# Turning LayerNorm rows and normalised queries with DMAs from on-chip memory instead of on TensorE, in the forward pairs of a linear-attention and gated-MLP training step

## The chip, the core and the metric

The kernel runs on one core of a Trainium2 chip. The metric is the device time of one execution in microseconds (us). A change of this kernel is told from no change at about 0.2%, some 2.2 us.

A core has five engines that work side by side and wait for each other through semaphores: TensorE (PE, with its weight loads shown as PEld), VectorE (DVE), ScalarE (ACT), GpSimd (POOL) and SyncE (SP). Here SP issues all DMAs, one after the other, in one queue: an issue that has to wait holds up the issues behind it.

## The reference

A forward pass of four layers and its backward pass, for 2048 tokens of width 512 in bf16. Layers 0 and 2 are linear attention with 32 heads of width 16, layers 1 and 3 a gated MLP of width 1376. Weights are shared between layers 0 and 2 and between layers 1 and 3.

```python
def _A_ref(x, wqkv, wo):
    q, k, v = ...                       # x @ wqkv, split into heads
    pq, pk = phi(q), phi(k)             # where(t > 0, t + 1, exp(t)) + 1e-6
    kv = jnp.einsum("bhsd,bhse->bhde", pk, v)
    z = jnp.einsum("bhsd->bhd", pk)
    num = jnp.einsum("bhqd,bhde->bhqe", pq, kv)
    den = jnp.einsum("bhqd,bhd->bhq", pq, z)[..., None] + 1e-6
    return (num / den reshaped to (B, S, D)) @ wo

def _B_ref(x, w_gate, w_up, w_down):
    g = x @ w_gate; u = x @ w_up
    return (_sigmoid(g) * u) @ w_down

x = x + _A_ref(_layernorm(x), A_wqkv, A_wo)
x = x + _B_ref(_layernorm(x), B_w_gate, B_w_up, B_w_down)
x = x + _A_ref(_layernorm(x), A_wqkv, A_wo)
x = x + _B_ref(_layernorm(x), B_w_gate, B_w_up, B_w_down)
```

The outputs are x and the gradients of x and of the five weight matrices.

## The kernel before

The 2048 tokens are 16 tiles of 128 (`st`, `NST` = 16). Each forward attention layer is done in `kq_fwd` up to its small matrix `M_sb`; what is left of it, the product of the normalised queries with `M_sb`, is woven into the MLP layer that follows, in `ab_fwd`. That function runs over pairs of tiles; its loop has `i` from 1 to 7 and `st = 2*i`, once for layer 1 and once for layer 3. The first pair stands ahead of the loop, written out tile by tile.

One round of the loop holds:

- `gu`, six times ("units" below): 8 matmuls on `wg` and 8 on `wu` for two 128-wide chunks of the MLP (the sixth has one chunk). They read `hT`, the LayerNorm rows of the pair turned so that the model width lies on the partitions. ScalarE takes two sigmoids from `g_ps` (into `ssd_t` and `oms`), DVE multiplies with `u_ps` into `hhT`, POOL writes the second half of `ssd_t`, and SP stores `ssd_t` to DRAM (`sv_ssd`) for the backward pass. `ssd_t` has five buffers in layer 1 and three in layer 3; the PSUM pools `g`, `u` and `t` have two banks each, `y` and `ln` one.
- `down_mm`, twice: 11 matmuls each, for the two tiles of the pair before.
- `attn_y(st + 2)` and `attn_y(st + 3)`: 4 matmuls each, of the turned queries `pqnT` with `M_sb`; DVE adds the result to `x`, and `ln_stats` (DVE, then three small operations on POOL) prepares the LayerNorm.
- `ln.apply(st + 2)` and `ln.apply(st + 3)`: ScalarE writes normalised rows into `hstage`, and SP stores both to DRAM (`sv_h`). `ln.stage_T` turns the two tiles with 8 TensorE transposes into a PSUM bank, and ScalarE copies them to `hT` for the next round.
- for the pair after the next: `pair_prod` (POOL), `pair_front1` and `pair_front2` (DVE: the denominators, their reciprocals and the normalised queries `pqnstage`, stored as `sv_pqn`) and `pair_front3`, 8 TensorE transposes and a ScalarE copy into `pqnT`.
- `after`: LayerNorm rows of the next layer, or the output. `trans`: DVE's block transposes of `hhT` into `tr_stg`, stored as `sv_hdd` and `sv_hdl`. `turn_weights`: transposing DMAs and stores for the weights of the backward pass, or their copies.

TensorE, ScalarE, DVE and POOL execute in the order in which the program is written. The SP queue alone is put in order by the scheduler of the language. Several helpers record operations for many callers; `transpose_blocks`, `evac_copy` and `ps_tile` are of this kind.

Of the kernel before, what the change touches and what calls it, by code (L numbers as in the profile page):

```python
# [9 lines left out]
BF16 = mybir.dt.bfloat16  # L10
# [12 lines left out]
P = 128  # L23
NST = S // P
NDC = D // P
# [363 lines left out]
def dram_batch(ap2d, b, nb=NB):  # L389
    return ap2d[batch_rows(b, nb), :].rearrange("(n p) d -> p n d", p=P)  # L390
# [141 lines left out]
class FwdLN:  # L532
# [10 lines left out]
        if st < NST:  # L543
            self.nmr[st] = ln_stats(self.k, self.k.xs[st][:], self.rstd(st), st < 1)

    def apply(self, st):
        if st >= NST:
            return
        k, nc, l = self.k, self.k.nc, self.l
        if st % 2 == 0:  # L550
            self.cur = k.lnres["stg"].tile([P, 2, D], BF16, name="hstage", tag="hstage")
        h_t = self.cur[:, st % 2, :]
        self.hs[st] = h_t
        ln_apply(k, k.xs[st][:], h_t, self.nmr.pop(st), self.rstd(st), st < 1)
        if st % 2 == 1:
            nc.sync.dma_start(out=dram_batch(k.sv[l]["h"], st // 2, 2), in_=self.cur[:])

# [341 lines left out]
def attn_fronts(k, A, pool, small):  # L899
    nc = k.nc  # L900
    sva = k.sv[A.l]
    cur, F_ = {}, {}
    A.F = F_

    def prod(st, eng=None):
        if st >= NST:
            return
        if st % 2 == 0:
            cur["prod"] = pool.tile([P, 2, D], BF16, name="prod2", bufs=1)
        F_[st] = dict(prod=cur["prod"][:, st % 2, :])  # L910
        (eng or nc.gpsimd).tensor_tensor(F_[st]["prod"], A.pq_all[:, st, :], A.zb[:], ALU.mult)

    def front1(st):
        if st >= NST:
            return
        F_[st]["den"] = small.tile([P, H], F32, name="den")
        nc.vector.tensor_reduce(F_[st]["den"][:], F_[st]["prod"].rearrange("p (h e) -> p h e", h=H), AX.X, ALU.add)

    def front2(st):
        if st >= NST:  # L920
            return
        if st % 2 == 0:
            cur["pqn"] = pool.tile([P, 2, D], BF16, name="pqnstage", bufs=2)
        f = F_[st]
        den = f["den"]
        f["pqn"] = cur["pqn"][:, st % 2, :]
        nc.vector.tensor_scalar(den[:], den[:], EPS, None, ALU.add)
        nc.vector.reciprocal(A.rden_all[:, st, :], den[:])
        nc.vector.tensor_tensor(f["pqn"].rearrange("p (h e) -> p h e", h=H),
                                A.pq_all[:, st, :].rearrange("p (h e) -> p h e", h=H),  # L930
                                A.rden_all[:, st, :].unsqueeze(2).to_broadcast([P, H, DH]), ALU.mult)
        if st % 2 == 1:
            nc.sync.dma_start(out=dram_batch(sva["pqn"], st // 2, 2), in_=cur["pqn"][:])

    def front3(st):
        if st >= NST:
            return
        f = F_[st]
        if st % 2 == 0:
            cur["T"] = pool.tile([P, 2, NDC, P], BF16, name="pqnT2", bufs=2)  # L940
        pqnT = cur["T"][:, st % 2, :, :]
        transpose_blocks(k, k.ps["ln"], pqnT, [f["pqn"][:, c * P:(c + 1) * P] for c in range(NDC)],
                         "scalar", tag="ln_tp")
        f["T"] = pqnT

    def pair_prod(i):
        if i >= NST // 2:
            return
        f = F_[2 * i] = dict(prod=pool.tile([P, 2, D], BF16, name="prod2", bufs=1))
        nc.gpsimd.tensor_tensor(f["prod"][:], A.pq_all[:, 2 * i:2 * i + 2, :],  # L950
                                A.zb[:].unsqueeze(1).to_broadcast([P, 2, D]), ALU.mult)

    def pair_front1(i):
        if i >= NST // 2:
            return
        f = F_[2 * i]
        f["den"] = small.tile([P, 2 * H], F32, name="den2", bufs=2)
        nc.vector.tensor_reduce(f["den"][:], f["prod"][:].rearrange("p n (h e) -> p (n h) e", h=H), AX.X, ALU.add)

    def pair_front2(i):  # L960
        if i >= NST // 2:
            return
        f = F_[2 * i]
        den = f["den"]
        pqn = pool.tile([P, 2, D], BF16, name="pqnstage", bufs=2)
        rden = A.rden_all[:, 2 * i:2 * i + 2, :].rearrange("p n h -> p (n h)")
        nc.vector.tensor_scalar(den[:], den[:], EPS, None, ALU.add)
        nc.vector.reciprocal(rden, den[:])
        nc.vector.tensor_tensor(pqn[:].rearrange("p n (h e) -> p (n h) e", h=H),
                                A.pq_all[:, 2 * i:2 * i + 2, :].rearrange("p n (h e) -> p (n h) e", h=H),  # L970
                                rden.unsqueeze(2).to_broadcast([P, 2 * H, DH]), ALU.mult)
        nc.sync.dma_start(out=dram_batch(sva["pqn"], i, 2), in_=pqn[:])
        f["pqn"] = pqn

    def pair_front3(i):
        if i >= NST // 2:
            return
        pqn = F_[2 * i]["pqn"]
        pqnT = pool.tile([P, 2, NDC, P], BF16, name="pqnT2", bufs=2)
        ps = ps_tile(k, "ln", [P, 2, NDC, P], BF16, "ln_tp")  # L980
        for j in range(2):
            for c in range(NDC):
                nc.tensor.transpose(ps[:, j, c, :], pqn[:, j, c * P:(c + 1) * P], k.ident[:])
        nc.scalar.copy(pqnT[:], ps[:])
        for j in range(2):
            F_[2 * i + j] = dict(T=pqnT[:, j, :, :])

    A.pair_prod, A.pair_front1, A.pair_front2, A.pair_front3 = pair_prod, pair_front1, pair_front2, pair_front3

    def attn_mm(st, bank="y"):  # L990
        if st >= NST:
            return
        pqnT = F_[st]["T"]
        y_ps = F_[st]["y"] = ps_tile(k, bank, [P, D], F32, "y_ps")
        for c in range(NDC):
            nc.tensor.matmul(y_ps[:], lhsT=pqnT[:, c, :], rhs=A.M_sb[:, c, :],
                             start=(c == 0), stop=(c == NDC - 1))

    def attn_add(st):
        if st >= NST:  # L1000
            return
        y_ps = F_.pop(st)["y"]
        res = k.xs[st][:] if A.x_src is None else A.x_src[:, st, :]
        nc.vector.tensor_tensor(k.xs[st][:], y_ps[:], res, ALU.add)
        A.ln.stats(st)

    def attn_y(st, bank="y"):
        attn_mm(st, bank)
        attn_add(st)

    A.attn_mm, A.attn_add = attn_mm, attn_add
    A.prod, A.front1, A.front2, A.front3, A.attn_y = prod, front1, front2, front3, attn_y
# [38 lines left out]
def ab_fwd(k, A, ln, fill, nxt=None, out_cb=None, bwd=None):  # L1051
# [3 lines left out]
    with ExitStack() as ctx:  # L1055
# [89 lines left out]
        A.pair_front1(2)  # L1145
        gu(1, 1, *CQUADS[1])
        ln.apply(3)
        A.pair_front2(2)
        A.pair_prod(3)
        down_mm(0)  # L1150
        gu(1, 1, *CQUADS[2])
# [5 lines left out]
        for i in range(1, NPAIR):  # L1157
            st = 2 * i
            last = i == NPAIR - 1
            nf = fill.share(i, NPAIR - 1)  # L1160

            def trs(n):
                for _ in range(min(n, len(pend))):
                    trans(*pend.pop(0))
            nt = 1 if i < NPAIR - 2 else 2
            gu(st, 2, *CUNITS[0])
            if l == 3 and i > 1:
                turn_weights()
            A.attn_y(st + 2, "t")
            A.pair_front1(i + 2)  # L1170
            after(st - 3)
            gu(st, 2, *CUNITS[1])
            A.attn_y(st + 3, "t")
            A.pair_front2(i + 2)
            trs(nt)
            fills((nf + 2) // 3)
            gu(st, 2, *CUNITS[2])
            if l == 3 or i % 2 == 0:
                turn_weights()
            if i > 1:  # L1180
                down_mm(st - 2)
            ln.apply(st + 2)
            if last:
                trans(NBLK - 1, 0)
            gu(st, 2, *CUNITS[3])
            if l == 3:
                turn_weights()
            down_mm(st - 1, "t")
            ln.apply(st + 3)
            A.pair_prod(i + 3)  # L1190
            fills(nf // 3)
            trs(nt)
            if last:
                trans(NBLK - 1, 1)
            gu(st, 2, *CUNITS[4])
            ln.stage_T([st + 2, st + 3], bank="t")
            A.pair_front3(i + 2)
            after(st - 2)
            gu(st, 2, *CUNITS[5])
            if l == 3:  # L1200
                turn_weights()
            fills((nf + 1) // 3, "vector")
            if l == 1 and last:
                nc.scalar.activation(k.tab[:], k.neg[:], ACT.Exp)
            if i % 2 == 1 and not last:
                pend += [(i // 2, g) for g in range(NG + 1)]
            if i == NPAIR - 3 and bwd is not None:
                bwd.load_g(0)
# [920 lines left out]
```

## Time and profile before

| | |
|---|---|
| median of three runs | 1115.92 us (1115.59 to 1117.04) |
| the profiled execution | 1115.54 us, span 1113.8 us, clock 0.998 |
| TensorE busy over the span | 98% |
| DVE, ACT, POOL busy | 65%, 44%, 42% |
| DMA | 265.63 MB, 238 GB/s on average |
| loop of layer 1 / of layer 3 | about 87 to 201 us / 280 to 396 us |
| 8 transposes of `hstage` or `pqnstage` on TensorE | the next operation starts 0.45 us later |
| SP's time for an issue of `sv_ssd` (median) | 0.36 us |
| DMA transposes in the kernel | all from DRAM: weights in the forward pass, `dqT_ld`, `pkT_ld`, `gT`, `p_set` and others in the backward pass |

In the timelines a line gives the start, the length, the engine, the line of the kernel, the operation, output and input. "SPq" lines are the issues of DMAs by SP, not the transfers. In tables of windows the columns are start and end, length, busy time of each engine with its number of instructions, the granted TensorE clock, the busy share of the DMA engines and the GB/s that they moved. The chain of waits of this profile is followed back only as far as 814 us.

### The profile page before, as it was taken

The page shows a single profiled execution, that of the slowest core. Times are in us where ns is not written, and L with a number is a line of the kernel's source. Part 1 is how long each engine was busy: PE and PEld are TensorE (multiplying, and loading weights), DVE is VectorE, ACT ScalarE, POOL GpSimd, SP SyncE. Part 2 cuts the span into 40 slices and gives each one's busy share as a digit, 9 for nine tenths or more (in the row PEclk, how much of TensorE's full clock was granted, in tenths as well). Part 3 has the DMA queues.
Part 4 walks back from the last instruction along what each step waited for, and adds up shares of the span by engine and source line. Part 5 has one row for each costly group of instructions (what it writes and reads, how often), then busy time and mean ns, then how long its engine had stood idle before and what let it go on. Part 6 is the DMA issues. An engine that isn't in the chain of part 4 may idle for free. (4 is left out here: it accounts for less than half of the span.)

```text
span 1113.8 us, 20048 instructions
## 1 busy us (share of the span) xinstructions
PE 1086.5 (98%) x7374; PEld 668.7 (60%) x7476; DVE 718.4 (65%) x1263; ACT 491.8 (44%) x914; POOL 467.9 (42%) x627
## 2 busy tenths in 40 slices
PE   7999999999999999999999999999999999999998
PEld 4467777546777754445666556544447756555587
DVE  7888897888678677767984640067678956632221
ACT  4776656556665623444643451234446513420001
POOL 3728776433766556774111430048771102420000
PEclk9999999999999999999999999999999999999999
DMA  7955767696776678976889978998868999958997
GB/s 218 320 173 164 206 192 216 197 257 208 210 230 201 205 223 303 299 242 227 245 247 272 255 218 279 282 311 259 221 204 232 272 263 264 258 188 278 271 264 165
DMA packets 353267, 265.63 MB, mean 238 GB/s; under 512 B 116304, under 2 KB 331792, under 8 KB 353168
## 3 DMA queue, kind: packets, MB, share of 16 engines
q1 hardware_dynamic: 353168, 264.35, 82.5%
q8 instruction: 58, 0.95, 0.3%
q14 instruction: 41, 0.34, 0.1%
HBM read 122.62 MB, written 119.47 MB: 217 GB/s over the span
## 5 line engine op out<-in xcount | busy, mean ns | idle before, releaser
L1717 PE MATMUL p_ps<-p_set,p_a 128*128 128x384 bf16 (+2 forms) x1792 | 264.4, 303 | 1.3 <-DMA p_set<-sv_hdd 0.8
L1717 PEld LDWEIGHTS <-p_a 128*128 128x128 bf16 x1792 | 168.8, 96 | 84.9 <-PE p_ps L1717 1.0
L1408 POOL TENSOR_TENSOR dd<-dhb,ssd 128x512 bf16<-128x512 bf16 x84 | 96.8, 1156 | 103.7 <-ACT dhb L1406 97.7
L1407 DVE TENSOR_TENSOR dd<-dhh_ps,ssd 128x512 bf16<-128x512 f32 x85 | 57.1, 678 | 120.6 <-ACT dhb L1406 116.4
L1432 PE MATMUL dh_ps<-wuT,dd 128*128 128x512 bf16 (+1 forms) x339 | 128.5, 379 | 1.2 <-DVE junk L1251 0.7
L1091 POOL TENSOR_TENSOR ssd_t<-hhT,oms 128x512 bf16<-128x512 bf16 (+1 forms) x92 | 99.7, 1091 | 59.5 <-DVE hhT L1090 33.0
L1432 PE MATMUL dh_ps<-wgT,dd 128*128 128x512 bf16 (+1 forms) x329 | 124.7, 379 | 0.1
L1432 PEld LDWEIGHTS <-dd 128*128 128x128 bf16 x680 | 66.3, 98 | 80.8 <-issue 1.5
L1406 ACT CAST dhb<-dhh_ps 128x512 bf16<-128x512 f32 x84 | 48.7, 588 | 116.8 <-PE dhh_ps L1400 105.4
L1732 DVE TENSOR_TENSOR dw_stg<-p_ps,dw_stg 128x384 bf16<-128x384 f32 (+2 forms) x76 | 32.2, 438 | 105.3 <-PE p_ps L1717 96.0
L1072 PE MATMUL g_ps<-hT,wg 128*128 128x256 bf16 (+1 forms) x792 | 92.8, 260 | 1.2 <-ACT hT L380 0.5
L1072 PE MATMUL u_ps<-hT,wu 128*128 128x256 bf16 (+1 forms) x792 | 92.8, 261 | 0.9 <-DVE hhT L1090 0.9
L1040 DVE STREAM_TRANSPOSE tr_stg<-dd 128x768 f32<-128x768 f32 (+1 forms) x62 | 86.9, 1438 | 4.9 <-DMA sv_hdd<-tr_stg 3.8
L1088 ACT ACTIVATE ssd_t<-g_ps 128x512 bf16<-128x512 f32 (+1 forms) x92 | 51.6, 561 | 78.5 <-PE g_ps L1072 57.4
L1090 DVE TENSOR_TENSOR hhT<-u_ps,ssd_t 128x512 bf16<-128x512 f32 (+1 forms) x92 | 57.8, 631 | 38.8 <-ACT ssd_t L1088 32.2
L1072 PEld LDWEIGHTS <-wg 128*128 128x128 bf16 x792 | 70.1, 98 | 20.8 <-issue 1.2
L1400 PE MATMUL dhh_ps<-gT,wdT 128*128 128x512 bf16 x299 | 77.0, 379 | 2.6 <-DVE dd L1407 1.9
L1107 PE MATMUL y_ps<-wd,hhT 128*128 128x512 bf16 (+1 forms) x337 | 77.7, 379 | 0.8
L1072 PEld LDWEIGHTS <-wu 128*128 128x128 bf16 x792 | 70.6, 98 | 8.4 <-issue 1.4
L1734 ACT CAST dw_stg<-p_ps 128x384 bf16<-128x384 f32 (+2 forms) x76 | 28.0, 385 | 84.5 <-PE p_ps L1717 81.1
L1400 PEld LDWEIGHTS <-wdT 128*128 128x128 bf16 x352 | 34.2, 98 | 43.8 <-issue 4.1
L517 POOL TENSOR_TENSOR rstd_all<-rstd_all,neghalf 128x1 f32<-128x1 f32 x64 | 38.0, 595 | 47.5 <-DVE rstd_all L516 42.9
(253 smaller groups left out, 1896.6 us busy)
## 6 DMA issues: line engine op xcount, KB each, us to landing
sv_hdd<-tr_stg SPq DMA_DIRECT2D x72, 384.0 KB, 4.7
p_set<-sv_hdd SPq DMA_DIRECT2D x18, 1536.0 KB, 7.0
sv_ssd<-ssd_t SPq DMA_DIRECT2D x74, 256.0 KB, 2.6
ssd<-sv_ssd SPq DMA_DIRECT2D x23, 768.0 KB, 5.3
h_ld<-sv_h SPq DMA_DIRECT2D x30, 256.0 KB, 4.1
sv_hdl<-tr_stg SPq DMA_DIRECT2D x24, 256.0 KB, 4.9
p_a<-sv_h SPq DMA_DIRECT2D x12, 512.0 KB, 6.4
p_set<-sv_hdl SPq DMA_DIRECT2D x24, 256.0 KB, 5.1
```

The source lines that it names most:

```text
L1040: nc.vector.transpose(t[:, :, 0:n * P].bitcast(F32).rearrange("p q (a j) -> p q a j", a=2 * n), src.rearrange("p c x -> p (c x)").bitcast( ...
L1072: nc.tensor.matmul(ps[:, ci * n:(ci + 1) * n], lhsT=w_sb[:, kc, (c0 + ci) * P:(c0 + ci + 1) * P], rhs=hT[:, kc, (st % 2) * P:(st % 2) * P ...
L1088: nc.scalar.activation(ssd[:, :, 0, :], gv, ACT.Sigmoid)
L1090: nc.vector.tensor_tensor(hh, uv, ssd[:, :, 0, :], ALU.mult)
L1091: nc.gpsimd.tensor_tensor(ssd[:, :, 1, :], hh, oms, ALU.mult)
L1107: nc.tensor.matmul(y_ps[:], lhsT=h[0:r, fc, off:off + P], rhs=k.wd[0:r, fc, :], start=(fc == 0), stop=(fc == NFC - 1))
L1400: nc.tensor.matmul(ps[:], lhsT=k.wdT[:, jc, u * P:(u + 1) * P], rhs=self.gT[B][:, jc, :], start=(jc == 0), stop=(jc == NDC - 1))
L1406: nc.scalar.copy(dhb[:], ps[:])
L1407: nc.vector.tensor_tensor(self.dd[ng][:, 0, c, :], ps[:], self.ssd[ng][:, c, 0, :], ALU.mult)
L1408: nc.gpsimd.tensor_tensor(self.dd[ng][:, 1, c, :], dhb[:], self.ssd[ng][:, c, 1, :], ALU.mult)
L1432: nc.tensor.matmul(self.acc[j][:], lhsT=dd[0:r, a, c, j * P:(j + 1) * P], rhs=w[0:r, u, :], start=(u == 0 and a == 0), stop=(u == NFC - 1 ...
L1717: nc.tensor.matmul(ps[:, 0:w], lhsT=lhs[:, s, ic * P:(ic + 1) * P], rhs=rhs, start=(s == 0), stop=(s == NST - 1))
```

## The change

In the loop of `ab_fwd` the turning of both operands goes from TensorE to DMAs. `ln.apply(..., True)` now issues, for each tile, a transposing DMA from `hstage` into `hT`, and `pair_front2` issues two from `pqnstage` into `pqnT`, one for each tile. `ln.stage_T` and `pair_front3` are no longer called in the loop, with their TensorE transposes, PSUM banks and ScalarE copies. Both `attn_y` stand behind the first unit, and both `ln.apply` behind the third unit and the first `down_mm`. Ahead of the loop nothing changes (`pair_front2(2, False)` keeps the TensorE path). The six `hT` pairs and five `pqnT` pairs that are made in the loop of each layer are concerned.

In SP's queue of the changed program a full pair reads: the stores of the first two units' `ssd_t`, two turns of `hstage`, two turns of `pqnstage`, `sv_pqn`, one `sv_hdd`, the third unit's store, and so on; in the first pair of each layer the second unit's store stands between the two turns of `hstage`.

```diff
@@ FwdLN
-    def apply(self, st):
+    def apply(self, st, turned=False):
...
             self.cur = k.lnres["stg"].tile([P, 2, D], BF16, name="hstage", tag="hstage")
+            if turned:
+                self.hTs[st // 2] = k.lnres["hT"].tile([P, NDC, 2, P], BF16, name="hT")
...
         ln_apply(k, k.xs[st][:], h_t, self.nmr.pop(st), self.rstd(st), st < 1)
+        if turned:
+            nc.sync.dma_start_transpose(out=self.hTs[st // 2][:, :, st % 2, :], in_=h_t)
@@ attn_fronts
-    def pair_front2(i):
+    def pair_front2(i, turned=True):
...
+        if turned:
+            pqnT = pool.tile([P, 2, NDC, P], BF16, name="pqnT2", bufs=2)
+            for j in range(2):
+                nc.sync.dma_start_transpose(out=pqnT[:, j, :, :], in_=pqn[:, j, :])
+                F_[2 * i + j] = dict(T=pqnT[:, j, :, :])
         nc.sync.dma_start(out=dram_batch(sva["pqn"], i, 2), in_=pqn[:])
@@ ab_fwd, ahead of the loop
-        A.pair_front2(2)
+        A.pair_front2(2, False)
@@ ab_fwd, in the loop
             A.attn_y(st + 2, "t")
+            A.attn_y(st + 3, "t")
             A.pair_front1(i + 2)
             after(st - 3)
             gu(st, 2, *CUNITS[1])
-            A.attn_y(st + 3, "t")
             A.pair_front2(i + 2)
...
             if i > 1:
                 down_mm(st - 2)
-            ln.apply(st + 2)
+            ln.apply(st + 2, True)
+            ln.apply(st + 3, True)
             if last:
                 trans(NBLK - 1, 0)
             gu(st, 2, *CUNITS[3])
...
             down_mm(st - 1, "t")
-            ln.apply(st + 3)
             A.pair_prod(i + 3)
...
             gu(st, 2, *CUNITS[4])
-            ln.stage_T([st + 2, st + 3], bank="t")
-            A.pair_front3(i + 2)
             after(st - 2)
```

## The prediction

> **What bounds the kernel now.** I read the busy shares on the page first. The span is 1113.8 us and the execution took 1115.54 us, so 1.74 us lie around it; the median shown is 1115.92 us.
>
> ```profile
> PE 1086.5 (98%) x7374; PEld 668.7 (60%) x7476; DVE 718.4 (65%) x1263; ACT 491.8 (44%) x914; POOL 467.9 (42%) x627
> ```
>
> TensorE is the bound over the whole span, but the change touches only the pair loops of layers 1 and 3 (about 87 to 201 us and 280 to 396 us). The chain of waits is followed back only to 814 us, so these stages have to be read from windows. Columns: length, then busy time of PE, PEld, DVE, ACT, POOL, granted clock, DMA share, GB/s.
>
> ```profile
> 120.00:137.00 17.00, 16.89 (x135) 12.46 (x135) 14.86 (x25) 10.61 (x19) 13.30 (x20) 1.00 0.72 229
> 344.00:362.00 18.00, 17.90 (x143) 13.27 (x143) 14.56 (x22) 10.88 (x19) 12.18 (x14) 1.00 0.63 197
> ```
>
> PE is busy for over 99% of both at full clock. Work taken off PE here is time won, as long as nothing else becomes late. The timeline of PE gives the price (start, length, operation):
>
> ```profile
> 117.56 0.61 PE L569 MATMUL ln_tp<-ident,hstage 128*128 128x128 bf16 x8
> 118.01 0.61 PE L983 MATMUL ln_tp<-ident,pqnstage 128*128 128x128 bf16 x8
> 118.46 0.60 PE L1072 MATMUL g_ps<-hT,wg 128*128 128x256 bf16 x4
> ```
>
> Lengths overlap, starts do not: eight transposes move PE on by 0.45 us. For what replaces them I looked at the transposing DMAs that the kernel already has: SyncE's time to issue one (min/median/max, ns), and how long it takes from issue to landing.
>
> ```profile
> L429 SPq DMA_TRANSPOSE wt_st<-in_A_wqkv_dram x4: 1331/1548/2049, 92.3 to 183.2; - x4
> ...
> L429 SPq DMA_TRANSPOSE wdT<-in_B_w_down_dram x2: 1835/2071/2307, 284.4 to 293.5; - x2
> ```
> ```profile
> L1927 SPq DMA_TRANSPOSE dqT_ld<-sv_dq x28: 1186/1270/2431, 591.4 to 968.1; - x28
> ...
> DMA to landing us min/median/max: 2.7/4.3/7.9
> ```
>
> All of them read DRAM. None in this trace reads on-chip memory, and that is the open price of this change. Where they would go in SP's queue (layer 3, a pair that starts at 329.87):
>
> ```profile
> 339.69 0.36 SPq L1094 DMA_DIRECT2D sv_ssd<-ssd_t  x1
> 341.86 0.36 SPq L972 DMA_DIRECT2D sv_pqn<-pqnstage  x1
> 343.35 0.52 SPq L1043 DMA_DIRECT2D sv_hdd<-tr_stg  x1
> 345.21 0.36 SPq L1094 DMA_DIRECT2D sv_ssd<-ssd_t  x1
> ```
>
> Between the second unit's store and the third's, SP has 5.5 us with two short issues in it.
>
> **Removed.** In the loop, `stage_T` turned 12 LayerNorm rows a layer (4 transposes each: 96 in both layers), and `pair_front3` turned 5 pairs of queries a layer (8 each: 80). The changed program has these 176 transposes and 176 weight loads fewer. 22 groups of 8 x 0.45 us = 9.9 us of PE, all of it in stages where PE is the bound: -9.9. ScalarE loses the two copies per pair (L380 1.01 us, L984 1.02 us); it has idle time, so they count nothing by themselves.
>
> **Added.** 24 turns of hstage rows and 20 of query rows, 128x512 each, all issued by SP. A full pair has four. Call SP's time for one c. A landing median of 4.3 us less an issue of 1.3 leaves about 3 us behind the issue; I use 2.7 (an estimate: 4.0 to landing is the median of the four wt_st turns, and their shortest issue is 1.33).
>
> **Moved.** Both attention products stand behind the first unit, so the second product, its DVE add and its statistics come 1.7 us earlier; on DVE and POOL they now stand ahead of the second unit's `hhT` (0.68) and `ssd_t` (1.16), which have two PSUM banks of slack. The second `apply` follows the first on ScalarE (0.81 us), ahead of the fourth unit's sigmoid, which waited 1.6 us for PE anyway. Cost zero; without that cover it is 0.8 us a pair.
>
> **When things are due.** A pair is 16.98 us now (329.87 to 346.85) and 16.1 without transposes. Counted from its first matmul: products end at 3.5; statistics on POOL (0.22+0.57+0.26 twice, behind the earlier ssd work that ends at about 5.4) give both rows at 7.9; the second apply ends at 8.9; the second unit's ssd is ready at 9.1 and its store, which stands ahead in SP's queue, takes 0.4. So the turns start at 9.5 (layer 1). The third one, at 9.5+2c, needs pqnstage, which is ready at 10.0 in layer 1 (112.3 against a start of 102.35) and at 12.0 in layer 3 (341.86 against 329.87). The last turn of the LayerNorm rows lands at 9.5+2c+2.7 and is due at 16.1: c may be 1.95. The last query turn lands at 9.5+4c+2.7 and is due at 18.7 (after the next pair's first unit and first product): c may be 1.62. In layer 3 ScalarE is held up by ssd stores, its apply ends at 9.9 (339.8) and the turns start at 10.2: c may be 1.6 for the rows and 1.45 for the queries. Beyond that, the queries turned in one pair hold the product that starts the next one, so the loop closes on itself with a period of 9.6+4c (9.5+4c+2.7, plus the product's 0.87, less the 3.5 at which the product ended a pair before), 0.7 more in layer 3. In layer 1 it equals today's 16.98 at c = 1.85.
>
> **Which c.** The nearest rows: dqT_ld has the same 128 KB and reads 1.27 at the median, wt_st (twice the bytes) stands in the very stage and reads 1.55. The lowest is 1.19, the highest of the forward stage 2.31 (wdT, 352 KB), the highest anywhere 5.93 (pkT_ld). I take 1.5, beside wt_st, and keep 1.19 and 5.93 as ends.
>
> [...]
>
> What the turns cost the transfers is the smaller matter. While pre_gT was turned, the DMA engines were just as full and moved less:
>
> ```profile
> 255.50:256.50 1.00, 1.00 (x12) 0.57 (x9) 0.79 (x2) 0.57 (x1) 0.00 (x0) 1.00 1.02 339
> ...
> 259.50:260.50 1.00, 1.00 (x12) 0.64 (x10) 0.97 (x2) 0.99 (x4) 0.00 (x0) 1.00 1.00 216
> ```
>
> At 216 GB/s the 0.52 MB of a pair fill the engines for 2.4 us of 16.1, which takes the share from 0.55-0.74 to 0.7-0.9: room, with stores landing somewhat later. [...]
>
> **What is given back at c = 1.5.** The first pair of each layer has no first `down_mm` and is 13.7 us long. In layer 1, LayerNorm rows land 0.5 late and queries 0.4: +0.9. In layer 3 that pair also has SP's wdT turn (2.31 us) behind the four; rows land 0.7 late, queries 0.4, and the third and fourth unit's ssd stores go out 3 to 4 us later than now. With three `ssd_t` buffers ScalarE's sigmoid already waits for such a store there:
>
> ```profile
> 299.70 0.60 ACT L1088 ACTIVATE ssd_t<-g_ps 128x512 bf16<-128x512 f32 x1 [2.49 <-DMA sv_ssd<-ssd_t]
> ```
>
> 2.7 us later, it holds a g bank for about 3 us of PE after its two banks of slack: +4.0 with the rest. In later pairs the third unit's store leaves at 15.3 now and at about 16.3 then, within that slack; only the turning is 0.2 late in four of them: +0.8.
>
> Sum: -9.9 + 0.9 + 4.0 + 0.8 = -4.2, so 1115.54 - 4.2 = 1111.3 us. With c = 1.2 and no stall it is 1105.6; this case's own range is 1105 to 1113.7.
>
> **Rivals.**
> 1. Turning eats the saving: c of 1.65 to 1.95, or the stores' delay reaching all pairs of layer 3 (9 waits of ScalarE for sv_ssd, 12.8 us in all, are there now; one more us in each of five pairs). 1113.7 to 1118. Chance 0.12.
> 2. An on-chip source costs SP more than a DRAM source. At 2.31 the period is 18.8: eight intervals lose 1.9 us, the two after the short pairs about 4.2, and layer 3 its 4.0: +27, 1142 us. It decides from c = 1.85. For it: only DRAM sources are shown, and rows under load reach 2 to 2.4. Against: DRAM turns of 128 KB and 256 KB cost the same. From c = 2 to 3.3 (period 22.8) this gives 1128 to 1180. Chance 0.30.
> 3. SP becomes the bound altogether, c over 3.3; at 4.95 (the worst gT row) the period is 29.4: +133, 1249 us. Chance 0.18.
>
> That the change does nothing is excluded by the 176 transposes that are gone.
>
> **How the numbers follow.** The forecast case has 0.40 and is the likeliest single one; the three rivals have the rest, and most of that is slower. A measurement of this kernel tells 0.2% (2.2 us) from no change. Faster 0.40; same 0.08 (most of rival 1); slower 0.52. The range runs from the full saving, 1105, to rival 2's end, 1180, and leaves out rival 3.
>
> **What would show it.** SP's duration of the turns with source hstage and pqnstage is the first thing to read: under 1.65 us the forecast stands, over 1.85 it falls. Then PE's idle time before `y_ps<-M_sb,pqnT` and before the first `g_ps` of a pair, which a late turn must end; the start-to-start time of a pair (16.1 against 9.6+4c); and ScalarE's wait for sv_ssd at about 300 us, 5 us or less. The prediction is wrong if PE waits in steady pairs, or if pairs stay at 17.0 with short turns, which would put the loss on DVE or POOL.

## The result, and the profile after

The changed kernel takes 1134.08 us (median of 4 runs, 1132.14 to 1137.55) against 1115.78 us for the kernel before in the same comparison: a ratio of 1.0157, with a 95% interval of 1.0138 to 1.0176. It is slower by some 18 us, where the prediction's likeliest case had it faster by 4. The profiled execution took 1132.14 us, with a span of 1130.4.

The busy shares on the page and two windows, one inside the pair loop of layer 1 and one in that of layer 3 (length, then PE, PEld, DVE, ACT, POOL, granted clock, DMA share, GB/s):

```profile
PE 1086.7 (96%) x7300; PEld 659.0 (58%) x7300; DVE 722.3 (64%) x1263; ACT 472.3 (42%) x892; POOL 463.6 (41%) x627
```
```profile
120.00:137.00 17.00, 16.37 (x121) 11.54 (x119) 15.58 (x24) 8.78 (x16) 12.26 (x20) 1.00 0.96 249
344.00:362.00 18.00, 14.99 (x102) 9.94 (x102) 13.62 (x20) 7.86 (x15) 9.95 (x12) 1.00 0.68 188
```

TensorE, which lacked 0.1 us of busy time in each of these windows before, is now idle by 0.6 us of 17 in layer 1 and by 3 us of 18 in layer 3. The starts of the attention products give the length of each pair:

| | layer 1, pairs in us | layer 3, pairs in us |
|---|---|---|
| before | 14.61, 16.98, 16.99, 16.98, 16.99 | 14.60, 17.56, 16.98, 17.07, 16.98 |
| after | 13.71, 16.58, 16.88, 16.75, 17.22 | 13.72, 23.48, 19.17, 20.49, 19.93 |

The first `dh_ps` matmul on `pre_dd`, which ends this part of the program, starts at 402.56 before and at 419.20 after: that is 16.64 us, all of the 16.6 by which the spans differ. Nothing is lost later, and layer 1 was 0.7 us earlier at its end (first `g_mm` of the next layer at 206.77, 207.43 before). The loss is in layer 3.

The first thing that the prediction wanted read is the time of a turn in SP's queue. The instructions of the row turn's line, and of the tile `pqnT`:

```profile
L558 SPq DMA_TRANSPOSE hT<-hstage x24: 1189/1216/1932, 96.1 to 394.9; - x24
...
DMA to landing us min/median/max: 2.4/2.6/4.2
```
```profile
L979 SPq DMA_TRANSPOSE pqnT<-pqnstage x20: 1216/1250/1258, 99.4 to 375.6; - x20
...
DMA to landing us min/median/max: 2.4/2.5/3.2
```

They are short: c is 1.22 to 1.25 us, below the 1.5 that I took. TensorE waits for a turned row in three places only, 4.5 us in all, and never for turned queries. What did become late is seen in the totals of waits of the whole run (us in all, times, the longest; the first line is that of the kernel before) and in ScalarE's timeline:

```profile
ACT ssd_t L1088 <- DMA sv_ssd<-ssd_t: 12.8, 9, 2.7
```
```profile
ACT ssd_t L1097 <- DMA sv_ssd<-ssd_t: 45.3, 22, 5.2
...
PE g_ps L1081 <- ACT oms L1098: 13.6, 9, 2.8
```
```profile
299.05 0.38 ACT L1097 ACTIVATE ssd_t<-g_ps 128x256 bf16<-128x256 f32 x1 [5.21 <-DMA sv_ssd<-ssd_t]
...
303.70 0.60 ACT L1097 ACTIVATE ssd_t<-g_ps 128x512 bf16<-128x512 f32 x1 [4.00 <-DMA sv_ssd<-ssd_t]
```

ScalarE's sigmoid waits until the store of an older `ssd_t` has landed: 45.3 us in 22 waits (36.0 of them in the loop of layer 3), where it was 12.8 us in 9, all in layer 3. While it waits it holds a g bank, and TensorE stops behind it (13.6 us in 9 waits for `oms`). SP's timeline shows where the stores stand (the pair whose first matmul starts at 317.20):

```profile
330.77 0.36 SPq L1103 DMA_DIRECT2D sv_ssd<-ssd_t  x1
331.23 1.21 SPq L558 DMA_TRANSPOSE hT<-hstage  x1
332.53 2.52 SPq L979 DMA_TRANSPOSE pqnT<-pqnstage  x2
335.11 0.57 SPq L981 DMA_DIRECT2D sv_pqn<-pqnstage  x1
335.80 0.54 SPq L1052 DMA_DIRECT2D sv_hdd<-tr_stg  x1
336.44 0.59 SPq L1103 DMA_DIRECT2D sv_ssd<-ssd_t  x1
```

The order given above for a full pair does not hold in all of layer 3: here, in the third pair, the second unit's store stands between the row turns.

The third unit's store goes out at 336.44, which is 19.2 us into its pair; it was 15.3 before. POOL has written this `ssd_t` at 335.16, so 1.3 us of the delay are SP's queue; the other 2.6 are an `ssd_t` that is itself late, in a pair whose first two sigmoids had waited 2.36 and 0.81 us for older stores. Read store by store from POOL's and SP's timelines over the loop of layer 3, the mean time from the end of POOL's write to the issue of the store went from 0.1 to 1.4 us, and the mean time from issue to landing from 3.1 to 3.4. The queue, more than the transfers, makes the buffers come free later.

TensorE's timeline, and the windows around its two longest stalls, show one thing more:

```profile
299.75 1.03 PE L1081 MATMUL g_ps<-hT,wg 128*128 128x256 bf16 x8 [2.33 <-ACT oms L1098]
300.62 1.44 PE L1081 MATMUL u_ps<-hT,wu 128*128 128x256 bf16 x8
304.84 1.87 PE L1081 MATMUL g_ps<-hT,wg 128*128 128x256 bf16 x8 [2.77 <-ACT oms L1098]
```
```profile
300.00:304.00 4.00, 2.07 (x16) 1.49 (x14) 0.00 (x0) 0.30 (x1) 0.67 (x1) 0.64 1.07 302
304.00:308.00 4.00, 3.16 (x16) 2.26 (x16) 3.53 (x7) 3.23 (x7) 2.22 (x4) 0.51 0.96 313
```

Behind the stalls the granted clock falls to 0.64 and 0.51, and eight matmuls of 128x256 take 1.87 us instead of 1.04.

### The profile page after: what moved, and what is told of

Same layout as the page of the kernel before. It is cut to its first block, busy times and chain, and to the rows that moved or that the text cites. A ratio compares the mean times of both kernels' runs of the same rounds, so it can differ in the third digit from the quotient of the medians.

```text
span 1130.4 us, 19855 instructions
## 1 busy us (share of the span) xinstructions
PE 1086.7 (96%) x7300; PEld 659.0 (58%) x7300; DVE 722.3 (64%) x1263; ACT 472.3 (42%) x892; POOL 463.6 (41%) x627
## 2 busy tenths in 40 slices
DMA packets 377201, 271.38 MB, mean 240 GB/s; under 512 B 140240, under 2 KB 355728, under 8 KB 377104
## 5 line engine op out<-in xcount | busy, mean ns | idle before, releaser
L1100 POOL TENSOR_TENSOR ssd_t<-hhT,oms 128x512 bf16<-128x512 bf16 (+1 forms) x92 | 102.1, 1116 | 81.5 <-DVE hhT L1099 66.4
L1439 PE MATMUL dh_ps<-wgT,dd 128*128 128x512 bf16 (+1 forms) x340 | 128.8, 379 | 0.0
L1081 PE MATMUL g_ps<-hT,wg 128*128 128x256 bf16 (+1 forms) x792 | 93.6, 262 | 18.9 <-ACT oms L1098 13.6
L1116 PE MATMUL y_ps<-wd,hhT 128*128 128x512 bf16 (+1 forms) x352 | 80.9, 379 | 0.0
L1098 ACT ACTIVATE oms<-g_ps 128x512 bf16<-128x512 f32 (+1 forms) x96 | 53.8, 560 | 14.9 <-POOL ssd_t L1100 14.9
```

Source lines behind the costliest of these rows:

```text
L1081: nc.tensor.matmul(ps[:, ci * n:(ci + 1) * n], lhsT=w_sb[:, kc, (c0 + ci) * P:(c0 + ci + 1) * P], rhs=hT[:, kc, (st % 2) * P:(st % 2) * P ...
L1098: nc.scalar.activation(oms, gv, ACT.Sigmoid, scale=-1.0)
L1100: nc.gpsimd.tensor_tensor(ssd[:, :, 1, :], hh, oms, ALU.mult)
L1116: nc.tensor.matmul(y_ps[:], lhsT=h[0:r, fc, off:off + P], rhs=k.wd[0:r, fc, :], start=(fc == 0), stop=(fc == NFC - 1))
L1439: nc.tensor.matmul(self.acc[j][:], lhsT=dd[0:r, a, c, j * P:(j + 1) * P], rhs=w[0:r, u, :], start=(u == 0 and a == 0), stop=(u == NFC - 1 ...
```

## Experiments

Four theories. **A**: in layer 3 the ssd stores stand behind the turns in SP's queue, and three `ssd_t` buffers (layer 1 has five) don't cover the delay. **B**: the moved order itself overloads DVE and POOL. **C**: the turned transfers slow all landings. **D** came later: the removed transposes were also cover, and without them TensorE meets DVE. Ratios are to the kernel before, run beside on the same chip; pairs are read as above. Single executions differ by several us in the layer between the two loops (from its first `g_mm` to the first attention product of layer 3's loop 75.0 us in the changed kernel and `e10`, 75.3 before, 81.4 in `e13`), so single times are used only for pairs and waits.

**One layer at a time, and the order alone.** `e1` and `e2` make the whole change in one layer (in the other the old places and transposes stay); `e3` keeps all transposes.

```diff
-            ln.apply(st + 2, True)
-            ln.apply(st + 3, True)
+            ln.apply(st + 2, l == 1)          # e1; l == 3 in e2; False in e3
+            if l == 1:                        # e1; l == 3 in e2; always in e3
+                ln.apply(st + 3, l == 1)
...
+            if l != 1:                        # e1; l != 3 in e2; always in e3
+                ln.stage_T([st + 2, st + 3], bank="t")
+                A.pair_front3(i + 2)
```

> Change made in layer 1 only; layer 3 keeps its order and its TensorE transposes. Theory A (in layer 3 the ssd stores stand behind four turns in SP's queue, and with three ssd_t buffers the sigmoids wait and hold the g banks): layer 1 has five buffers, so the kernel is 0.5 to 2 us faster than before, about 1115. Theory B (the moved order, two products and two applies together, overloads DVE and POOL): layer 1 loses as well, 1117 to 1122. Theory C (the turns' 128 KB transfers in short packets slow every landing): like B, as the DMA share in layer 1 is the higher of the two.

> Change made in layer 3 only. Theory A: the whole loss is here, pair starts of layer 3 some 19 to 20 us apart, 1131 to 1135 us. Theories B and C: about half of the loss, 1122 to 1128.

> Only the order is changed in both layers: both attention products behind the first unit and both applies behind the third; all 176 TensorE transposes stay, no turn by DMA. Theory A: 1115 to 1118, pair starts 17.0 us apart, ScalarE's waits for sv_ssd within a few us of before's 12.8. Theory B: most of the loss is here, 1125 to 1135, with pairs of 18 us and more. Theory C: as before, 1115 to 1117.

`e1`: 1.0004 (0.9988 to 1.0021). `e2`: 1.0147 (1.0111 to 1.0183), with pairs of 23.72, 16.73, 19.56 and 20.00 behind the first. `e3`: 1.0013 (1.0001 to 1.0025); its pairs are 16.98 to 17.6 in layer 1, and 18.38 then 16.99 in layer 3. So the loss is in layer 3, as A wants, and B falls with `e3`. C is not settled by these runs, since five buffers in layer 1 would cover slower landings as well as later issues. The order costs about 1.5 us (0.1 to 2.8), which I had put at zero. And no gain is seen in layer 1 (-1.3 to +2.3 us), where A wanted 0.5 to 2.

**The number of buffers, both ways.** `e4` gives layer 3 a fourth buffer, `e5` takes two from layer 1.

```diff
-name="ssd_t", bufs=5 if more else 3)
+name="ssd_t", bufs=5 if more else 4)          # e4, with pqnstage bufs=1 in layer 3
+name="ssd_t", bufs=3)                         # e5
```

> The changed kernel with four ssd_t buffers in layer 3 instead of three; the room comes from pqnstage, one buffer instead of two in that layer. Theory A: ScalarE's waits for sv_ssd fall from 45 us to under 15, layer 3's pairs come to 16.5 to 17.5 us, 1113 to 1120 us in all, and the granted clock stays at 1.00 at 300 to 308 us. Theory B: unchanged, 1130 to 1135. Theory C: a few us at most, 1127 to 1132, since the transfers stay as slow.

> The changed kernel with three ssd_t buffers in layer 1 instead of five (layer 3 as changed, three). Theory A (stores behind the turns in SP's queue, too few buffers to cover them): layer 1 now falls ill like layer 3, pair starts 18 to 20 us apart instead of 16.6 to 17.2, ScalarE waits for sv_ssd there, 1140 to 1150 us. If the number of buffers were not what sets layer 3 apart: 1132 to 1136, layer 1 as before.

`e5`: 1.0379 (1.0357 to 1.0401), 25 us above the changed kernel; layer 1's pairs are 21.98, 22.78, 19.85 and 23.43, and the wait that matters has grown to

```profile
ACT ssd_t L1097 <- DMA sv_ssd<-ssd_t: 73.9, 29, 5.3
```

Nothing but the buffers was changed, so too few of them, with the turns in the program, is what makes a layer ill. (Three buffers in layer 1 without turns were not run; the kernel before has three in layer 3, with pairs of 17.0 to 17.6.) `e4`: 1.0089 (1.0053 to 1.0124), which is 0.7% under the changed kernel and less than A expected; ScalarE's waits came to 37.0 us and not under 15. Its pairs in layer 3 are 26.26, 16.65, 17.10 and 18.01: the later ones recover, but in the second SP has the query turns ahead of the row turns, and TensorE waits 6.4 us for `hT`.

**The place in the queue.** `e7` puts the query turns behind the row turns and the third unit's store; `e6` does that and issues the ssd stores of layer 3 from ScalarE's queue, each after the sigmoids of the second unit behind it; `e8` has that in both layers and four buffers.

```diff
+    def pair_turn(i, ins):                    # called after ln.apply(st + 3, True)
+        for j in range(2):
+            with k.tc.issue_after(ins):       # ins: the row turn
+                ins = nc.sync.dma_start_transpose(out=pqnT[:, j, :, :], in_=pqn[:, j, :]).ins
...
-                gu.ins = nc.sync.dma_start(out=sv["ssd"]...
+                late.append(put)              # e6, e8: put(nc.scalar), two units later
```

> The changed kernel, three ssd_t buffers in layer 3, but there the ssd stores are issued from ScalarE's queue (each behind the sigmoids of the second unit after it), and the query turns stand behind the row turns in SP's queue. All transfers are still there, turned ones too; only the place of the stores in SP's queue is gone. Theory A: PE's waits for oms fall under 4 us, layer 3 pairs of 16.5 to 17.5, 1114 to 1120 us. Theory C (the turned transfers themselves slow the stores): waits for sv_ssd stay over 25 us and the time at 1126 or more. The stores' issue on ScalarE may cost up to 2.5 us a pair there, beside its idle time.

> Four ssd_t buffers in layer 3 as in the run before, and the query turns placed behind the row turns in SP's queue (and behind the store of the third unit), where they had come ahead in the second pair of layer 3 and made PE wait 6.4 us for hT. Theory A: that wait goes, 1119 to 1123 us. If it is the transfers' load that makes hT late there, it stays, 1126 to 1130.

> All of it: ssd stores from ScalarE's queue in both layers, four ssd_t buffers in layer 3, query turns behind row turns. Theory A: no store waits behind a turn, pairs of 16.3 to 16.9 us in both layers, 1107 to 1114 us, below the kernel before. Theory C: 1118 or more.

`e6`: 1.0206 (1.0180 to 1.0231). `e7`: 1.0126 (1.0100 to 1.0152). `e8`: 1.0105 (1.0075 to 1.0135). All missed. With three buffers a store that is issued two units later is late by itself: `e6` keeps 29.5 us of ScalarE's waits in layer 3, so it says nothing between A and C. In `e7` those waits fall to 8.9 us there, but TensorE then waits 9.3 us for turned queries. Both also spoil layer 1, whose buffers they leave alone: its attention products wait 7.8 us (`e6`) and 5.6 us (`e7`) for queries that are turned late, with pairs of up to 20.51 and 19.90. In `e8` layer 3 has pairs of 16.4 to 17.4 behind the first, but TensorE waits 6.1 us for `hT` in layer 1: SP's row turn stands behind the store of a `wt_st` tile, which by the program needs the tile's own turn (4.0 us to landing at the median in the kernel before). Rearranging the queue moves the wait from ScalarE's buffers to TensorE's operands; SP's time has to become less.

**No turn at all, and fewer turns.** `e9` leaves turning out. `e10` turns two rows in one instruction, with `hT` laid out by row.

```diff
-            nc.sync.dma_start_transpose(out=pqnT[:, j, :, :], in_=pqn[:, j, :])    # j = 0, 1
+            nc.sync.dma_start_transpose(out=pqnT[:].rearrange("p n c t -> p (n c) t"),
+                                        in_=pqn[:].rearrange("p n d -> p (n d)"))  # e10
+            F_[2 * i + j] = dict(T=A.T0[:, j, :, :])                               # e9
```

> In the loops of layers 1 and 3 nothing is turned at all, neither by TensorE nor by a DMA: the units and the attention products read the first turned rows and queries again (turning is the part left out), all other work, waits and stores of the changed kernel stay. Theory A (the saving of 9.9 us is there, and what eats it is SP's queue): pairs of 16.1 to 16.3 us in both layers, 1106 to 1109 us. Theory D (where the transposes are gone TensorE meets DVE, which is busy 15.5 of 16.9 us in layer 1, so much of the saving does not exist): layer 1 stays at 16.6 to 16.9 a pair with PE waiting for hhT, 1109 to 1114 us.

> The changed kernel with two turns of 128x1024 a pair instead of four of 128x512: both rows' LayerNorm output in one, both rows' queries in one (hT laid out by row for it). Same bytes; SP's time for the turns falls from 4.9 us a pair to some 3.1, if one costs 1.55 like the wt_st turns of that size. Theory A: the stores behind them come 1.8 us earlier, layer 3's pairs fall from 19.2-20.5 to 17.5-18.5, 1121 to 1127 us. Theory C (the transfers): no change, 1131 to 1135.

`e9`: 0.9986 (0.9966 to 1.0006), which is not told from the kernel before, without any turning. That fits D. In layer 1 its pairs are 16.56, 16.84, 16.58 and 16.85, and TensorE waits for DVE:

```profile
136.12 1.03 PE L1080 MATMUL u_ps<-hT,wu 128*128 128x256 bf16 x8 [0.59 <-DVE hhT L1098]
```

`e9` keeps the moved order, which by itself made two of layer 1's pairs 0.4 and 0.6 us longer in `e3`, with TensorE waiting for `hhT` too. How much of D is the lost cover and how much the order, no run separates.

In layer 3 two of its pairs have the forecast length (16.09, 16.13) and one takes 17.37, but the second takes 20.88: behind a first pair that is 0.9 us shorter, the stores behind `wdT`'s turn go out no earlier than before (296.28, 295.86), and the clock falls again. That the wait for them also ends 2 us later than before is not explained.

```profile
302.88 1.87 PE L1080 MATMUL g_ps<-hT,wg 128*128 128x256 bf16 x8 [3.08 <-ACT oms L1097]
```
```profile
302.00:306.00 4.00, 3.12 (x17) 2.27 (x17) 3.49 (x7) 3.43 (x8) 2.22 (x4) 0.57 0.95 318
```

`e10`: 1.0041 (1.0028 to 1.0054), 1.2% under the changed kernel with the same bytes. A joint turn costs SP hardly more than a single one, 1.29 us at the median against 1.22 to 1.25:

```profile
L558 SPq DMA_TRANSPOSE hT<-hstage x12: 1231/1287/1435, 97.1 to 383.4; - x12
```

Two of 1.29 us are 2.6 us of SP a pair instead of 4.9. In layer 3 the mean time from POOL's write to the issue of a store falls from 1.4 to 0.7 us, while that from issue to landing stays at 3.4. This is what tells A from C: the landings did not get faster, and three quarters of the loss went. Layer 1's pairs (16.57, 16.84, 16.59, 16.85) are those of `e9` to 0.01 us: in them turning is hidden altogether. Layer 3's still lose (22.73, 16.78, 19.29, 17.54).

**Towards a good version.** `e11`: layer 1 only, joint turns, and DVE's block transposes ahead of the down product's add. `e12`: that, and in layer 3 joint turns from the third pair on, with four `ssd_t` buffers.

```diff
+            trs(nt)
             down_mm(st - 1, "t")
             A.pair_prod(i + 3)
             fills(nf // 3)
-            trs(nt)
...
+            ln.apply(st + 2, l == 1 or i > 2)         # e12; l == 1 in e11
```

> Layer 1 only, with two joint turns a pair; and DVE's second block transposes of a pair stand ahead of the second down product's add (where DVE waits for TensorE) instead of behind it, so that the fifth unit's hhT need not wait for them. Layer 3 as before. Theory D: the waits for hhT in layer 1 go, pairs of 16.2 to 16.5 us, 1111.5 to 1114 us. Without D: as with layer 1 alone, 1115 to 1117.

> As the run before, and in layer 3 too from the third pair on (its first two pairs, which also carry wdT's turn, keep TensorE's transposes), with four ssd_t buffers and one pqnstage there. Theory A: layer 3's later pairs at 16.3 to 17.0, so 0 to 2.5 us below the run before, 1109 to 1114 us. If the queue still makes stores late: pairs of 17.5 and more there, 1114 to 1119.

`e11`: 0.9997 (0.9985 to 1.0009): layer 1's pairs do fall, to 16.57, 16.32, 16.58 and 16.32, so DVE's order was part of it; but the time does not follow. In layer 3, where only DVE's order is new, the second and third pair take 18.81 and 17.24 (17.56 and 16.98 before). `e12`: 0.9958 (0.9943 to 0.9972), faster than both kernels, 1114.32 us against 1119.22. Windows of its later pairs in layer 3, whole pairs each:

```profile
313.83:329.92 16.09, 16.09 (x120) 11.54 (x118) 13.91 (x21) 8.95 (x18) 10.47 (x13) 1.00 0.88 254
329.92:346.01 16.09, 16.09 (x120) 11.54 (x118) 14.14 (x20) 7.99 (x16) 10.78 (x15) 1.00 0.94 264
346.01:362.10 16.09, 16.09 (x120) 11.54 (x118) 13.58 (x20) 8.29 (x16) 8.85 (x13) 1.00 0.84 247
```

TensorE is never idle, with the turned transfers in place and the DMA engines 0.84 to 0.94 busy: the transfers do no harm here. C is right that landings get slower (the median from issue to landing of `sv_ssd` at 283 to 395 us is 3.6 us here, 3.2 in the changed kernel, 3.0 before and 2.6 in `e9`), but not as the main cause. How much these tenths cost with three buffers is not shown.

**Taking the good version apart.** `e13`: its two side edits without any turn. `e14`: three buffers. `e15`: single turns. `e16`: turning from layer 3's first pair.

```diff
-name="ssd_t", bufs=5 if more else 4)
+name="ssd_t", bufs=5 if more else 3)                 # e14, with two pqnstage
...
-            ln.apply(st + 2, l == 1 or i > 2)
+            ln.apply(st + 2, False)                  # e13, with transposes and order of before
+            ln.apply(st + 2, True)                   # e16
```

> The kernel before, with its TensorE transposes and its order, and only two edits of the good version: four ssd_t buffers with one pqnstage in layer 3, and DVE's second block transposes of a pair ahead of the second down product. If turning by DMA is what earns the good version's gain: 0.5 to 1 us below before (layer 3's second pair 17.0 instead of 17.6), pairs of 17.0, 1114 to 1116. If the edits earn it: within 1 us of the good version's ratio of 0.9958.

> The good version with three ssd_t buffers (and two pqnstage) in layer 3. Theory A: ScalarE waits for sv_ssd again, over 25 us instead of 13.8, layer 3's later pairs 17 to 18.5 instead of 16.09, 4 to 10 us slower than the good version. If the joint turns alone are enough: within 1 us of it.

> The good version with four turns of 128x512 a pair instead of two of 128x1024 (4.9 us of SP a pair). Theory A with four buffers to cover: layer 3's later pairs 16.1 to 16.8, and 0 to 4 us slower than the good version. If the time of the turns in SP's queue decides even with four buffers: pairs of 17 and more, 4 to 8 us slower.

> The good version, but turning in the first two pairs of layer 3 too, where SP also issues wdT's turn and its two stores. Theory A: there the stores stand behind those as well, the second pair takes 19 us and more, TensorE stalls by 3 us or more and its granted clock drops after that (to 0.5 to 0.9 at 300 to 310 us); 3 to 7 us slower than the good version. If these pairs are no special case: 1 us faster than it.

| | ratio, 95% interval | layer 3, pairs behind the first | ScalarE's waits for sv_ssd |
|---|---|---|---|
| `e12` | 0.9958 (0.9943 to 0.9972) | 16.98, 16.09, 16.09, 16.09 | 14.7 us |
| `e13` | 1.0025 (1.0014 to 1.0035) | 16.98, 16.99, 16.98, 16.98 | 0.8 us |
| `e14` | 1.0090 (1.0076 to 1.0103) | 19.02, 16.54, 19.90, 18.46 | 25.8 us |
| `e15` | 1.0074 (1.0058 to 1.0090) | 16.98, 16.09, 18.76, 18.78 | 31.8 us |
| `e16` | 0.9990 (0.9979 to 1.0001) | 23.43, 17.08, 16.09, 16.09 | 8.5 us |

`e14` and `e15` lose more than either of their expectations had it; `e13`, expected below the kernel before, is above it; `e16` fits A. In this version the fourth buffer is worth 1.3% (0.0132 between the ratios, 15 us) and the joint turns 1.2% (13 us). These prices belong to this version: `e10` also has three buffers and joint turns, from the first pair of layer 3 on and in DVE's old order, and stands at 1.0041, below `e14`. The edits alone, without turning, make the kernel slower, with pairs of up to 17.91 in layer 1, where only DVE's order is new; so the gain comes from turning, and DVE's new order pays only together with it. In layer 3's crowded first pairs turning still costs 0.3%: SP's row turn stands behind a query turn, three stores and a weight load, and TensorE waits for it.

```profile
306.56 2.12 SPq L979 DMA_TRANSPOSE pqnT<-pqnstage  x1
...
311.78 1.63 SPq L558 DMA_TRANSPOSE hT<-hstage  x1
```
```profile
316.05 1.86 PE L1083 MATMUL g_ps<-hT,wg 128*128 128x256 bf16 x8 [5.21 <-DMA hT<-hstage]
```
```profile
312.00:316.00 4.00, 0.00 (x0) 0.00 (x0) 0.72 (x2) 0.00 (x0) 2.84 (x3) 0.88 1.15 350
316.00:320.00 4.00, 3.73 (x17) 2.64 (x19) 0.28 (x1) 1.59 (x3) 0.00 (x0) 0.50 1.10 333
```

## Why the prediction was wrong

**The step that failed** is in "What is given back": "In later pairs the third unit's store leaves at 15.3 now and at about 16.3 then, within that slack". So the late store was priced at nothing (the +0.8 beside it is for turns that land 0.2 us late). The later pairs of layer 3 are 2.2 to 3.4 us longer than before, where 0.9 shorter was wanted, and the store left at 19.2 (pair from 317.20). The 16.3 is a slip, too: it goes with layer 1's start of the turns, 9.5. With layer 3's 10.2 the prediction's own rows give 10.2 + 4 x 1.5 + 0.36 + 0.52 = 17.1. But at the measured c the same sum comes to about 16.2, so the slip is not what failed. I had added the turns to the queue once, and set the one us that came out against TensorE's slack. But the wait closes on itself: a late landing delays a sigmoid, that delays `ssd_t` and the applies, and these delay the next stores and the next turns, which in the pair from 335.84 start at 15.4 instead of 10.2. The prediction wrote such a loop down for the turned queries (period 9.6+4c) and not for the stores, though ScalarE already waited 12.8 us for them; a loop that is already waiting has no slack to give. Rival 1 named this mechanism and priced it at one us a pair, with a chance of 0.12.

**The first pairs of layer 3** (+4.0) had the right mechanism and too small a size. ScalarE's wait was forecast at about 5 us near 300; it was 5.21 and then 4.00. The second pair took 23.48 us, where it was 17.56: TensorE stalled by 2.33 and 2.77, and what is left above 16.1, some 2.3 us, is the clock: 5.23 us of busy time at about 0.56 do the work of 2.9. In `e9` a good half of the growth (to 20.88) comes without any turn. The fall of the clock was in no row that I had read.

**The saving** (-9.9) is of the right size where nothing else binds: 16.09 against a forecast of 16.1 in three pairs of `e12`. In layer 1 a third of it exists (16.56 to 16.85 in `e9`, where 16.98 should have come to 16.1). The window that I showed had DVE 14.86 of 17.00 busy, and I read from it that TensorE is the bound; set against 16.1 it is 92%, and after the change it was 15.58. The transposes behind the fifth unit gave DVE the time for its block transposes before the next `u_ps` bank was wanted; that `e11` wins back 0.5 us in every second pair, by moving these, fits, though it does not show that the transposes were what covered them. What layer 1 then gains is mostly given back behind it in the execution profiled of `e12`: its last product starts 3.3 us earlier than before (168.92, 172.25) and layer 3's first one only 0.5 earlier (282.23, 282.69), with TensorE waiting in between 1.8 us for the last `hT` and 2.4 us for DVE's `pk_all` and `pq_all` (none and 0.9 before). Since single executions differ there (75.0 to 81.4 us, above), and `e10` kept 1.8 of 2.3 us, this is one reading and not shown.

**c** was 1.5 and measured 1.22 to 1.25; the estimate of 2.7 to landing behind it was twice too long, since 2.5 to 2.6 is the time from the start of the issue, some 1.3 us behind its end. Both errors were on the safe side. Rivals 2 and 3, with 0.48 of the chances, are refuted: an on-chip source cost SP 1.22 to 1.25 us at the median, no more than the DRAM rows (1.27 for `dqT_ld`, 1.55 for `wt_st`). In SP's time hardly any growth with the size is seen here: a turn of 128x1024 took 1.29 us in `e10` and one of 128x512 took 1.22. The prediction made c the first thing to read and said that under 1.65 the forecast stands. That was the wrong test: c was well under, and the forecast fell by the other sign that it named, ScalarE's waits.

**Moved at cost zero**: 1.5 us by `e3` (1.0013), with pairs of 17.4 and 17.6 in layer 1 and 18.38 in layer 3. TensorE waits 1.5 us for `hhT` in layer 1 there (0.9 before), so the cover named was too thin. **+0.9 in layer 1's first pair** did not come (13.71 long, no wait for `hT`); instead the last rows were late, by 1.85 us at 187.21, behind a `wt_st` turn of 1.66 us in SP's queue.

## What to carry to other kernels

When instructions are put into an in-order DMA queue, go through the stores behind them, ask which buffers those free, and look whether somebody already waits for these: such a wait is a loop without slack, and a delay in it is paid in every round and not once (here 2.2 to 3.4 us in each later pair of layer 3). Before work is taken off the engine that bounds a stage, set every other engine's busy time against the shorter stage, and look for what the removed work was covering. And make the queue's work less (two turns in one, another buffer) before rearranging it: in three runs another order only changed which engine waited.

## What the runs showed of the hardware

- A turning DMA from on-chip memory cost SP nearly the same at two sizes: 1.22 us for 128x512 and 1.29 us for 128x1024 (medians, bf16; single ones were longer, such as 2.12 in `e16`, of the larger size). Counted from the start of the issue the larger landed after 3.2 to 3.4 us in `e10`, the smaller after 2.5 to 2.6 in the changed kernel (medians).
- Some stalls of TensorE cost more than their length. After stalls of 2.33 and 2.77 us in the changed kernel, of 3.08 in `e9` and of 5.21 in `e16`, the granted clock in the next windows was 0.64 and 0.51, 0.57, and 0.50, and eight matmuls of 128x256 took up to 1.91 us instead of 1.04. They also took up to 1.91 after stalls of 4.10 us in `e10` and 4.32 in `e5`. The length alone does not decide. After 2.02 us in `e14` the second and third eight took 1.70 and 1.91 us, while after 2.09 in the changed kernel, 2.13 and 2.24 in `e15` and 2.86 in `e2` they took 1.03 to 1.04, as they did after 1.83 us in the changed kernel and 1.88 in `e15`. Ahead of layer 3's loop, sixteen matmuls of 128x128 took 1.64 and 1.91 us instead of 1.06 behind a stall of 1.61 us in `e13`.
- The 44 turns of 128 KB added 23,936 packets of under 512 bytes (140240 against 116304), 544 a turn; the 22 joint turns of `e10` added 1056 each. If the count has a part that grows with the bytes and one for each turn, these two figures give, as an estimate, 512 packets for every 128 KB (256 bytes each, if they are alike) and 32 for each turn.
- The `sv_pqn` stores issued right behind turns in the changed kernel took SP 0.57 us each; 0.36 is the median of the kernel before.
